# Keys in another order and V in longer runs, with one transposed tile moved from TensorE to the DMA queue in every second head

## The chip, the cores and the metric

The kernel runs on one core of a Trainium2 chip. The metric is the device time of one execution in microseconds, from the first to the last instruction of the core with what lies around them; lower is better. "TensorE", "VectorE", "ScalarE" and POOL (GpSimd) are the four engines that compute, each with a queue of its own that is worked off in order; SP (SyncE) only issues DMAs, also in order. In the profile they are PE (with PEld for the loads of weights), DVE, ACT, POOL and SP.

## What is computed

A conditioned transformer block on a sequence of 2048 rows of 640 values, bf16 in and out. Six vectors are made from a condition `c`; two of them scale and shift a layer norm ahead of each half of the block, and one gates each half's result. The first half is attention with 32 heads of 128 against a given cache of 2048 keys and values; the second mixes neighbouring rows and runs an MLP.

```python
mod = (silu(c) @ w_mod)                        # sa, ca, ga, sb, cb, gb
h = layernorm(x) * (1 + ca) + sa
q = (h @ wq)                                   # 2048 x (32 heads x 128)
p = softmax(q @ k_cache^T * 128 ** -0.5)       # per head: 2048 x 2048
x = x + ga * ((p @ v_cache) @ wo)
h = layernorm(x) * (1 + cb) + sb
x = x + gb * B(h)                              # row shifts, two matmuls, layer norms, a GELU MLP
```

The sum over keys doesn't depend on the order in which the keys are taken, so long as K, P and V agree on it. The change lies in the attention.

## The kernel before

All instructions are listed in one order by a small recorder (`Prog`); it finds, for each operation, which earlier ones it must wait for (from the keys in `r=` and `w=`) and gives each engine its part of the list, in that order. A wait therefore holds up whatever stands behind it on the same engine. DMAs named "sync" go to SP's queue, those named "gpsimd" to POOL's.

The attention is a software pipeline over 512 steps: step `s` is head `h = s // 16` and query tile `j = s % 16` (128 queries). In each step:

- TensorE multiplies the query tile with all 2048 keys, in two halves of 1024 (`qk`, L286), into the PSUM tile `Sps`. VectorE scales each half into the SBUF tile `negS` (three buffers) and takes its minimum (L559). POOL joins the two minima (L569), and ScalarE takes the exponential of 2048 scores into a P buffer, `ring<-negS` (L572). There are eight P buffers (`RPB`) and twelve for transposed P (`RPT`).
- P has to be transposed so that keys lie on partitions. For 14 of a head's 16 tiles a DMA transpose does it, issued from SP (`transpose`, L222): tiles (0,1), (4,5), (6,7), (8,9), (12,13) and (14,15) in pairs, tiles 2 and 11 alone. Tiles 3 and 10 (`PE_TILES`) are transposed by TensorE against an identity, in two halves of eight blocks, spread over the steps three and four later (`t_piece`, L253). The halves are copied out of PSUM by ScalarE (L262), except the second half of tile 3, which VectorE copies (L264, `by_dve`).
- Eleven steps behind (`PVD`; eight at the very end) TensorE multiplies transposed P with V (`pv`, L299): 16 products per tile, one per 128 keys, summed in PSUM. V is kept with a column of ones behind each 128 values, so that column 128 of the sum is the softmax's denominator. ScalarE copies two tiles' sums at once to `Of` (L550).
- Four steps further POOL takes the power -1 of four denominators (`rcp`, L440), multiplies (`norm`, L447) and sends four tiles to a scratch in DRAM with a DMA of its own (L454).
- Between these, TensorE makes the next head's queries in 20 pieces (`q_piece`, L237, copied by ScalarE at L244).

K, V and the query weights of a head are double buffered and loaded from SP's queue, between the transposes in the order of the list: K of the next head at tile 2 (a DMA transpose, L205), the weights at tile 6 (L209), V of the next head at tile 12 (L214). In V's buffer partition p holds the keys t x 128 + p, sixteen runs of 128 values at a pitch of 130.

After the attention the scratch is read back transposed (L495) and the second part of the block follows; the change doesn't touch it.

Of the kernel before, what the change touches and what calls it, by code (L numbers as in the profile page):

```python
# [115 lines left out]
def bass_adaLN_cond__mha_block_cached__mixer_s_mlp__prompt_kernel(  # L116
# [21 lines left out]
    with ExitStack() as es:  # L138
# [11 lines left out]
        if True:  # L150
            with ExitStack() as es1:
# [9 lines left out]
                kv = sb1("kv", [128, 2 * SK + 2 * NKT * 130 + 2 * KT * 128 + 2 * SQ], BF16)  # L161
                small = sb1("small", [128, 4 * NQT + 32], F32)
                hTx = sb1("hTx", [128, US], BF16)
# [4 lines left out]
                rstd = small[:, 3 * NQT:4 * NQT]  # L168
                nm0, nm1, nm, rl = [small[:, 4 * NQT + 8 * i:4 * NQT + 8 * i + 8] for i in range(4)]
                hT = hTx[:, 0:KT * SQ].rearrange("p (k q) -> p k q", k=KT)  # L170
# [3 lines left out]
                KTs = kv[:, 0:o1].rearrange("p (b s) -> p b s", b=2)  # L174
                Vaug = kv[:, o1:o2].rearrange("p (b k d) -> p b k d", b=2, k=NKT)
                wq = kv[:, o2:o3].rearrange("p (b k d) -> p b k d", b=2, k=KT)
# [26 lines left out]
                def load_k(h):  # L203
                    hb = h % 2
                    G.dma("sync", lambda e: e.dma_start_transpose(KTs[:, hb], A_k_cache[0, h]), ("k", hb), w=[("KT", hb)])  # L205

# [5 lines left out]
                def load_v(h):  # L212
                    hb = h % 2
                    G.dma("sync", lambda e: e.dma_start(Vaug[:, hb, :, 0:128], A_v_cache[0, h].rearrange("(t p) d -> p t d", p=128)),  # L214
                          ("v", hb), w=[("V", hb)])
# [49 lines left out]

                by_dve = lambda g, r: r == 1 and g % NQT == PE_TILES[0]

# [24 lines left out]
                def pv(g, half):  # L292
                    hb = (g // NQT) % 2
                    b = g % RPT
                    ob = PO[:, ((g // 2) % 2) * 512 + (g % 2) * 130:]

                    def f(t):
                        for kt in range(half * 8, half * 8 + 8):
                            ins = t.matmul(ob[:, 0:129], PTs[:, b, kt, :], Vaug[:, hb, kt, 0:129],  # L299
                                           start=(kt == 0), stop=(kt == NKT - 1))  # L300
                        return ins
                    G.op("tensor", f, r=[("PT", b, half), ("V", hb), "ones"], w=[("O", (g // 2) % 2)])

# [28 lines left out]
                if H > 1:  # L332
# [89 lines left out]
                mone = small[:, 0:4]  # L422
                G.op("gpsimd", lambda g: g.memset(mone, -1.0), w=["mone"] + [("mv", t) for t in range(NQT)])
                bank(("q", 0, NQC - 1))
# [13 lines left out]
                def rcp(gr):  # L438
                    b = gr % 2
                    G.op("gpsimd", lambda g: g.tensor_tensor(  # L440
                        out=rl[:, 4 * b:4 * b + 4], in0=Of[:].rearrange("p a z d -> p (a z) d")[:, 4 * b:4 * b + 4, 128],
                        in1=mone, op=ALU.pow),
                         r=[("Of", 2 * b), ("Of", 2 * b + 1), "mone"], w=[("rl", b)])

                def norm(gr, z):
                    b = gr % 2
                    G.op("gpsimd", lambda g: g.tensor_scalar(  # L447
                        out=On[:, b, z, :], in0=Of[:, 2 * b + z // 2, z % 2, 0:128],
                        scalar1=rl[:, 4 * b + z:4 * b + z + 1], scalar2=1.0, op0=ALU.mult, op1=ALU.mult),
                        r=[("Of", 2 * b + z // 2), ("rl", b)], w=[("On", b, z)])  # L450
# [393 lines left out]
```

## Time and profile before

| | |
|---|---|
| median of 3 runs | 1614.81 us (1610.35 to 1619.43) |
| the profiled execution | 1604.1 us, span 1602.3 us |
| mean granted TensorE clock | 0.993 |
| attention, first score reduction to last exponential | 35.5 to 1253.9 us |
| projection after it, first matmul (L631) | from 1269.6 us |
| TensorE, weight loads, VectorE, ScalarE, POOL busy | 1492.6, 963.0, 1392.5, 1288.2, 622.8 us |
| DMA queue of SP | 1,161,424 packets, 314.59 MB |

The profile is of one execution. Busy time of an engine is the union of its instructions' spans. The page cuts the span into 40 equal slices and gives a busy digit for each engine in each (9 is 90% or more); the DMA digit is the mean over 16 DMA engines, whose packets overlap, so that a share can exceed 1. A group row gives source line, engine, operation, the tiles written and read, the shape and count, then busy time and mean duration. A wait row says who waited for whom, for how long in total, how often, and the longest. A row of a stretch gives its length, then busy time and count for each engine, the granted clock, the DMA share and GB/s. A row of SP's timeline gives the start of an issue and the time for which the queue was occupied with it (merged over several: x2), not the transfer, which ends later ("to landing").

### The profile page before, as it was taken

Reading aid. Unit: us, or ns where it says so; the run is one execution under the profiler, and the core shown is the slowest. Engines: PE = TensorE matmul, PEld = TensorE weight load, DVE = VectorE, ACT = ScalarE, POOL = GpSimd, SP = SyncE. Lnnn points to the kernel's source line nnn. Section 1 sums busy time; section 2 is a strip of 40 time slices with the busy share of each in tenths; the row PEclk is TensorE's granted clock in tenths of the full one; section 3 lists DMA queues with packets and bytes.
Section 4 is the critical chain, followed back from the end, with each engine's and each line's share of the span. In section 5 each row is a group of like instructions: output and inputs, shape, how many; then the busy total and the mean of one; then the engine's idle time right before and its main releaser. Section 6 shows DMA issues by size and latency. Waiting matters only on the chain.

```text
span 1602.3 us, 34804 instructions
## 1 busy us (share of the span) xinstructions
PE 1492.6 (93%) x13978; PEld 963.0 (60%) x14231; DVE 1392.5 (87%) x2460; ACT 1288.2 (80%) x1145; POOL 622.8 (39%) x1394
## 2 busy tenths in 40 slices
PE   5799999999999999999999999999999799999998
PEld 3466666666666666666666666666666555545444
DVE  6999999999999999999999999999999266666424
ACT  4999999999999999999999999999999300055330
POOL 0144444444444444444444444444444423322000
PEclk9999999999999999999999999999999899999999
DMA  9999999999999999999999999999999994530000
GB/s 305 229 230 239 238 243 237 253 241 240 237 237 233 239 237 237 239 239 247 243 250 246 250 239 235 246 228 239 236 244 244 241 196 106 106 111 1 17 17 34
DMA packets 1167730, 333.62 MB, mean 208 GB/s; under 512 B 1148304, under 2 KB 1161552, under 8 KB 1167568
## 3 DMA queue, kind: packets, MB, share of 16 engines
q1 hardware_dynamic: 1161424, 314.59, 98.3%
q0 software_dynamic: 6144, 16.79, 3.3%
q8 instruction: 112, 1.84, 0.5%
q14 instruction: 50, 0.41, 0.1%
HBM read 43.48 MB, written 19.40 MB: 39 GB/s over the span
## 4 chain that ended last, share of the span: by engine, by line
DVE 30%; ACT 24%; PE 20%; DMA 15%; issue 10%; POOL 0%; SPq 0%; ACTq 0%; DVEq 0%
DVE negS L559 27%; ACT ring L572 19%; DMA ring<-ring 13%; PE Sps L631 8%; PE Sps L772 4%; PE Oaug L756 2%; PE QPp L756 2%; ACT ring L262 2%; ACT Of L550 2%; PE Sps L741 1%; ACT kv L244 1%; DMA ring<-in_A_x_dram 1%; DVE ring L364 1%; DMA negS<-o_scratch 1%; PE Sps L286 1%
## 5 line engine op out<-in xcount | busy, mean ns | idle before, releaser
L559 DVE TENSOR_SCALAR_CACHE_REDUCE negS<-Sps 128x1024 f32<-128x1024 f32 x1024 | 1177.2, 1220 | 22.2 <-PE Sps L286 12.5
L572 ACT ACTIVATE ring<-negS,small 128x2048 bf16<-128x2048 f32 x512 | 1011.4, 2029 | 21.9 <-DMA ring<-ring 15.7
L299 PEld LDWEIGHTS PTp<-kv,ring 128*128 128x128 bf16 x8192 | 560.0, 98 | 245.0 <-DMA ring<-ring 6.7
L286 PE MATMUL Sps<-kv 128*128 128x512 bf16 x1949 | 596.3, 383 | 62.8 <-DVE negS L559 42.9
L299 PE MATMUL PTp<-kv,ring 128*128 128x129 bf16 x8192 | 645.6, 221 | 6.5 <-DMA ring<-ring 5.6
L569 POOL TENSOR_SCALAR small<-small 128x1 f32<-128x1 f32 x512 | 145.8, 285 | 621.5 <-DVE negS L559 621.4
L286 PEld LDWEIGHTS Sps<-kv 128*128 128x128 bf16 x2048 | 124.5, 97 | 187.2 <-DVE negS L559 158.0
L447 POOL TENSOR_SCALAR On<-Of,small 128x128 bf16<-128x128 f32 x512 | 189.8, 371 | 13.0
L669 ACT COPY kv<-PTp 128x640 bf16<-128x640 bf16 x32 | 22.0, 692 | 155.0 <-PE PTp L666 154.9
L440 POOL TENSOR_TENSOR small<-Of,small 128x4 f32<-128x4 f32 x128 | 133.2, 1040 | 6.3 <-ACT Of L550 6.2
L454 POOL DMA_DIRECT2D o_scratch<-On x128 | 103.1, 806 | 40.8 <-POOL On L447 37.2
L237 PE MATMUL Oaug<-hTx,kv 128*128 128x512 bf16 x265 | 101.2, 387 | 7.9 <-ACT ring L262 4.2
L550 ACT COPY Of<-PTp 128x259 f32<-128x259 f32 x256 | 99.5, 389 | 10.5 <-PE PTp L299 10.5
L237 PE MATMUL QPp<-hTx,kv 128*128 128x512 bf16 x259 | 97.5, 381 | 2.5 <-ACT hTx L391 1.8
L559 DVE DVE_READ_ACCUMULATOR negS<-Sps 128x1 f32 x1024 | 85.4, 83 | 0.0
L612 POOL TENSOR_SCALAR On<-On 128x1 f32<-128x1 f32 x48 | 24.3, 507 | 152.9 <-DVE On L621 152.9
L639 DVE TENSOR_TENSOR ring<-Sps,mod_bc 128x640 f32<-128x640 f32 x16 | 13.2, 825 | 77.0 <-PE Sps L631 77.0
L631 PE MATMUL Sps<-wo,hTx 128*128 128x128 bf16 (+1 forms) x504 | 71.8, 304 | 5.0 <-DMA hTx<-o_scratch 4.7
L776 DVE TENSOR_TENSOR ring<-Sps,ring 128x640 f32<-128x640 f32 x16 | 13.2, 825 | 66.2 <-PE Sps L772 66.2
L631 PE MATMUL Sps<-wo,negS 128*128 128x128 bf16 (+1 forms) x504 | 69.1, 298 | 1.3 <-DMA negS<-o_scratch 0.9
L262 ACT COPY ring<-Oaug 128x1024 bf16<-128x1024 bf16 x64 | 66.2, 1034 | 0.0
L631 PEld LDWEIGHTS Sps<-wo,hTx 128*128 128x128 bf16 x512 | 40.2, 99 | 36.9 <-DMA hTx<-o_scratch 4.5
(82 smaller groups left out, 1011.2 us busy)
## 6 DMA issues: line engine op xcount, KB each, us to landing
kv<-in_A_v_cache_dram SPq DMA_DIRECT2D x32, 512.0 KB, 5.2
o_scratch<-On POOLq DMA_DIRECT2D x128, 128.0 KB, 4.5
ring<-in_A_x_dram SPq DMA_DIRECT2D x8, 640.0 KB, 4.9
kv<-in_A_wq_dram SPq DMA_DIRECT2D x32, 160.0 KB, 3.6
wo<-in_A_wo_dram SPq DMA_DIRECT2D x1, 5120.0 KB, 16.4
ring<-ring SPq DMA_TRANSPOSE x256, 7.1
ring<-in_w_mod_dram SPq DMA_DIRECT2D x1, 3200.0 KB, 13.6
out_dram<-wo SPq DMA_DIRECT2D x16, 160.0 KB, 1.8
```

The costliest lines, as they stand in the source:

```text
L237: G.op("tensor", lambda t: t.matmul(JB[jb], wq[:, hb, q, :], hT[:, q, cc * 512:(cc + 1) * 512], start=(q == 0), stop=(q == KT - 1)), r=[(" ...
L262: G.op("scalar", lambda a: a.copy(dst, src), r=[("J", jb)], w=[("PT", g % RPT, r)])
L286: ins = t.matmul(Sps[:, col:col + 512], QT[:, hb, j * 128:(j + 1) * 128], KTs[:, hb, col:col + 512], start=True, stop=True)
L299: ins = t.matmul(ob[:, 0:129], PTs[:, b, kt, :], Vaug[:, hb, kt, 0:129], start=(kt == 0), stop=(kt == NKT - 1))
L440: G.op("gpsimd", lambda g: g.tensor_tensor(out=rl[:, 4 * b:4 * b + 4], in0=Of[:].rearrange("p a z d -> p (a z) d")[:, 4 * b:4 * b + 4, 128 ...
L447: G.op("gpsimd", lambda g: g.tensor_scalar(out=On[:, b, z, :], in0=Of[:, 2 * b + z // 2, z % 2, 0:128], scalar1=rl[:, 4 * b + z:4 * b + z ...
L454: G.dma("gpsimd", lambda e: e.dma_start(o_scr[jj // 2:jj // 2 + 2, :, hh].rearrange("a p z d -> p a (z d)"), On[:, b].rearrange("p (a z) d ...
L550: G.op("scalar", lambda a, p=p: a.copy(Of[:, p % 4].rearrange("p z d -> p (z d)")[:, 0:259], PO[:, (p % 2) * 512:(p % 2) * 512 + 259]), r= ...
L559: G.op("vector", lambda v, half=half, s=s, r8=r8: v.tensor_scalar(out=negS[:, s % 3, half * 1024:(half + 1) * 1024], in0=Sps[:, half * 102 ...
L569: G.op("gpsimd", lambda g, r8=r8: g.tensor_scalar(out=nm[:, r8:r8 + 1], in0=nm0[:, r8:r8 + 1], scalar1=nm1[:, r8:r8 + 1], scalar2=None, op ...
L572: G.op("scalar", lambda a, s=s, r8=r8: a.activation(Pb[:, s % RPB, :], negS[:, s % 3, :], ACT.Exp, bias=nm[:, r8:r8 + 1], scale=-1.0), r=[ ...
L631: ins = t.matmul(YB[b][:, c0:c0 + cw], OTj[pr % 2][:, 2 * hh + z, :], wo[:, hh, c0:c0 + cw], start=(hh == 0), stop=(hh == H - 1))
```

## The change

Keys are taken in the order 16 p + c: partition p holds sixteen consecutive keys, and key tile c is the keys 16 p + c. K is transposed from a view of 128 rows of 4 KB, V is loaded in eight runs of two keys (512 bytes) per partition, at a pitch of 260 elements, with two ones ahead of each run and two behind it. Even key tiles multiply [1, V] (129 columns, starting on element 1 of the run's slot), odd ones [V, 1] with a result one column further on, so that V's sums meet in columns 1 to 128, and the sums of ones end up in two columns, 0 and 129. Because these two columns start at different products, the first key tile needs all 130 columns written: a copy of its V with a one ahead and a zero behind is kept in a small buffer `V0`, made by POOL once per head at tile 2, ahead of that step's other POOL work. POOL adds the two sums before the power.

In the odd heads tile 3 is no longer transposed by TensorE; tiles 2 and 3 go as one pair by DMA. Tile 10 stays with TensorE in all heads. VectorE copies the second half of tile 3 in every fourth head alone (0, 4, 8, ...); where TensorE transposes it in the other even heads, ScalarE copies it.

```diff
-                small = sb1("small", [128, 4 * NQT + 32], F32)
+                small = sb1("small", [128, 4 + 130 + 2 + 32], F32)
+                V0 = small[:, 4:134].bitcast(BF16).rearrange("p (b d) -> p b d", b=2)
-                Vaug = kv[:, o1:o2].rearrange("p (b k d) -> p b k d", b=2, k=NKT)
+                Vaug = kv[:, o1:o2].rearrange("p (b k d) -> p b k d", b=2, k=NKT // 2)
...
-                    G.dma("sync", lambda e: e.dma_start_transpose(KTs[:, hb], A_k_cache[0, h]), ("k", hb), w=[("KT", hb)])
+                    G.dma("sync", lambda e: e.dma_start_transpose(
+                        KTs[:, hb].rearrange("p (c q) -> p c q", c=NKT), A_k_cache[0, h].rearrange("(q c) d -> q (c d)", c=NKT)), ("k", hb), w=[("KT", hb)])
...
-                    G.dma("sync", lambda e: e.dma_start(Vaug[:, hb, :, 0:128], A_v_cache[0, h].rearrange("(t p) d -> p t d", p=128)),
+                    G.dma("sync", lambda e: e.dma_start(Vaug[:, hb, :, 2:258], A_v_cache[0, h].rearrange("(p t z) d -> p t (z d)", t=NKT // 2, z=2)),
...
-                is_pe = lambda g: g % NQT in PE_TILES
+                is_pe = lambda g: g % NQT in PE_TILES[(g // NQT) % 2:]
...
-                by_dve = lambda g, r: r == 1 and g % NQT == PE_TILES[0]
+                by_dve = lambda g, r: r == 1 and g % NQT == PE_TILES[0] and (g // NQT) % 4 == 0
...
-                            ins = t.matmul(ob[:, 0:129], PTs[:, b, kt, :], Vaug[:, hb, kt, 0:129],
+                            ins = t.matmul(ob[:, 0:130] if kt == 0 else ob[:, kt % 2:kt % 2 + 129], PTs[:, b, kt, :],
+                                           V0[:, hb] if kt == 0 else Vaug[:, hb, kt // 2, (1, 130)[kt % 2]:(130, 259)[kt % 2]],
...
-                G.op("gpsimd", lambda g: g.memset(Vaug[:, :, :, 128:130], 1.0), w=["ones"])
+                for c0 in (0, 258):
+                    G.op("gpsimd", lambda g, c0=c0: g.memset(Vaug[:, :, :, c0:c0 + 2], 1.0), w=[("ones", c0)])
...
+                G.op("gpsimd", lambda g: g.memset(V0[:, :, 0:1], 1.0), w=["v0o"] + SMK)
+                G.op("gpsimd", lambda g: g.memset(V0[:, :, 129:130], 0.0), r=["v0o"], w=["v0e"])
...
                     G.op("gpsimd", lambda g: g.tensor_tensor(
-                        out=rl[:, 4 * b:4 * b + 4], in0=Of[:].rearrange("p a z d -> p (a z) d")[:, 4 * b:4 * b + 4, 128],
-                        in1=mone, op=ALU.pow),
+                        out=rl[:, 4 * b:4 * b + 4], in0=Og[:, :, 0], in1=Og[:, :, 129], op=ALU.add),
+                         r=[("Of", 2 * b), ("Of", 2 * b + 1)], w=[("rs", b), ("rl", b)])
+                    G.op("gpsimd", lambda g: g.tensor_tensor(
+                        out=rl[:, 4 * b:4 * b + 4], in0=rl[:, 4 * b:4 * b + 4], in1=mone, op=ALU.pow),
...
+                    if s < NG and j == 2:
+                        G.op("gpsimd", lambda g, hb=h % 2: g.tensor_scalar(
+                            out=V0[:, hb, 1:129], in0=Vaug[:, hb, 0, 2:130], scalar1=1.0, scalar2=1.0, op0=ALU.mult, op1=ALU.mult),
+                            r=[("V", h % 2), "v0e"], w=[("V0", h % 2)])
...
-                            Of[:, p % 4].rearrange("p z d -> p (z d)")[:, 0:259], PO[:, (p % 2) * 512:(p % 2) * 512 + 259]),
+                            Of[:, p % 4].rearrange("p z d -> p (z d)")[:, 0:260], PO[:, (p % 2) * 512:(p % 2) * 512 + 260]),
```

More of the change, by code (lines that the diff above doesn't have):

```diff
@@ L168, in bass_adaLN_cond__mha_block_cached__mixer_s_mlp__prompt_kernel @@
                 rstd = small[:, 3 * NQT:4 * NQT]
-                nm0, nm1, nm, rl = [small[:, 4 * NQT + 8 * i:4 * NQT + 8 * i + 8] for i in range(4)]
+                nm0, nm1, nm, rl = [small[:, 136 + 8 * i:136 + 8 * i + 8] for i in range(4)]
+                V0 = small[:, 4:134].bitcast(BF16).rearrange("p (b d) -> p b d", b=2)
                 hT = hTx[:, 0:KT * SQ].rearrange("p (k q) -> p k q", k=KT)
@@ L422, in bass_adaLN_cond__mha_block_cached__mixer_s_mlp__prompt_kernel @@
                 mone = small[:, 0:4]
-                G.op("gpsimd", lambda g: g.memset(mone, -1.0), w=["mone"] + [("mv", t) for t in range(NQT)])
+                SMK = [("mv", t) for t in range(NQT)] + [("rstd", cc) for cc in range(NQC)]
+                G.op("gpsimd", lambda g: g.memset(mone, -1.0), w=["mone"] + SMK)
+                G.op("gpsimd", lambda g: g.memset(V0[:, :, 0:1], 1.0), w=["v0o"] + SMK)
+                G.op("gpsimd", lambda g: g.memset(V0[:, :, 129:130], 0.0), r=["v0o"], w=["v0e"])
                 bank(("q", 0, NQC - 1))
@@ L447, in norm @@
                     G.op("gpsimd", lambda g: g.tensor_scalar(
-                        out=On[:, b, z, :], in0=Of[:, 2 * b + z // 2, z % 2, 0:128],
+                        out=On[:, b, z, :], in0=Of[:, 2 * b + z // 2, z % 2, 1:129],
                         scalar1=rl[:, 4 * b + z:4 * b + z + 1], scalar2=1.0, op0=ALU.mult, op1=ALU.mult),
```

5 lines of the change are left out of this document (3 added, 2 removed).

## The prediction

> **What bounds the kernel now.** I read the page's head, then the same two stretches of the attention stage by engine, then the queue that issues the DMAs, then the rate of the DMA engines in short stretches, then waits and groups.
>
> The page, busy shares and DMA queues:
>
> ```profile
> PE 1492.6 (93%) x13978; PEld 963.0 (60%) x14231; DVE 1392.5 (87%) x2460; ACT 1288.2 (80%) x1145; POOL 622.8 (39%) x1394
> DMA  9999999999999999999999999999999994530000
> q1 hardware_dynamic: 1161424, 314.59, 98.3%
> q8 instruction: 112, 1.84, 0.5%
> ```
>
> Two stretches of one head each (heads 8 and 12), busy time by engine, clock, DMA share, GB/s:
>
> ```profile
> 337.70:374.90 37.20, 35.78 (x368) 24.22 (x372) 37.20 (x68) 37.20 (x32) 17.44 (x40) 1.00 1.19 245
> 488.70:527.40 38.70, 36.55 (x371) 24.89 (x376) 37.59 (x67) 36.95 (x31) 17.71 (x41) 1.00 1.26 231
> ```
>
> In head 8 VectorE and ScalarE are never idle; in head 12 both idle 1.1 to 1.8 us, and the head is longer. The first score reductions of successive heads stand 37.22 us apart in heads 1 to 9, and 37.84 on average over heads 1 to 31. So a second thing limits. SP's queue, heads 12 and 13 (start, duration):
>
> ```profile
> 525.69 6.72 SPq L222 DMA_TRANSPOSE ring<-ring  x2
> 532.46 0.59 SPq L214 DMA_DIRECT2D kv<-in_A_v_cache_dram  x1
> 533.09 18.47 SPq L222 DMA_TRANSPOSE ring<-ring  x4
> 551.61 2.01 SPq L205 DMA_TRANSPOSE kv<-in_A_k_cache_dram  x1
> 553.66 4.58 SPq L222 DMA_TRANSPOSE ring<-ring  x1
> 558.29 0.59 SPq L209 DMA_DIRECT2D kv<-in_A_wq_dram  x1
> 558.92 11.00 SPq L222 DMA_TRANSPOSE ring<-ring  x3
> ```
>
> Each row ends where the next begins (0.04 us between). The trace has this in every head from 1 on, and each transpose is issued long after the exponential that it needs: 3 to 11 us late in heads 9 to 30. From head 2's V load (issued at 112.95) to head 31's (1214.42) the queue takes 37.98 us per head and is never short of work. It sets the pace; the engines catch up and then wait:
>
> ```profile
> ACT ring L572 <- DMA ring<-ring: 15.7, 26, 1.7
> POOL small L569 <- DVE negS L559: 621.4, 508, 9.0
> DMA to landing us min/median/max: 4.5/5.2/6.3
> 535.24 0.28 POOL L569 TENSOR_SCALAR small<-small 128x1 f32<-128x1 f32 x1 [1.67 <-DVE negS L559]
> ```
>
> (The third line is the V load's, L214; the fourth is POOL's minimum for tile 2 of head 13.) What the queue's engines do in short stretches:
>
> ```profile
> 37.00:45.00 8.00, 7.17 (x34) 3.05 (x32) 3.81 (x7) 6.98 (x7) 0.59 (x2) 1.00 1.06 395
> 1288.00:1290.00 2.00, 1.96 (x33) 1.77 (x31) 0.01 (x1) 0.00 (x0) 0.00 (x0) 1.00 1.27 290
> 193.15:194.15 1.00, 1.00 (x12) 0.58 (x10) 1.00 (x3) 1.00 (x1) 0.62 (x2) 1.00 1.36 225
> 190.15:191.40 1.25, 1.25 (x13) 0.76 (x13) 1.25 (x3) 1.25 (x2) 0.65 (x3) 1.00 0.57 9
> ```
>
> These are 1280-byte packets (wo), 256-byte packets of a transpose from DRAM, 256-byte packets of a V load, and a stall of some 1.5 us just after a 16 KB instruction fetch (112 fetches in all, row q8). A tile's transpose is 524288 bytes: 1.81 us at 290 GB/s.
>
> **The change part by part.** Base: the profiled execution, 1604.1 us (span 1602.3). It is 0.7% below the median of the runs, 1614.8; I put the sum on the median. 0.5%, about what a measurement can tell, is 8 us.
>
> *Tile 3 of the 16 odd heads goes by DMA.* A single transpose (tile 2) becomes a pair (2, 3), the number of issues stays. 16 x 1.81 = +29.0 us on the queue. Upper end: the stage's own average including stalls, 38.0 us for 14 tiles, K, V and a third of a tile, 2.33 us each, +37. It can't be below 1.81, the fastest rate seen. The stalls follow instruction fetches and not bytes, so I take +29. Tile 2 now lands with tile 3, some 2 us later, while its product comes 11 tiles on and its P buffer has 2.8 us to spare in the heads that the queue limits: nothing.
>
> *V in 512-byte runs*, 1024 packets instead of 2048. Per packet and engine, 290 GB/s is 16 x 256 / 290 = 14.1 ns, 395 GB/s is 51.8 ns for 1280 bytes; the line between gives 23.5 ns at 512 and 1.51 us for a V load. Today its data move at 225 GB/s, 2.33 us, with a dip of a few tenths behind it where transposes follow a plain load, which stays. Ends: nothing saved (time goes by bytes), or 1.43 us (a 512-byte packet costs what one of 256 does, 0.90). With today's slowness kept, 1.51 x 290/225 = 1.95 us, it saves 0.38, without it 0.82; I take 0.5, as writes at a 520-byte pitch are as ragged as those at 260. 32 loads less the first, which is before the stage: -16 us (0 to -44).
> The Trainium skill, "DMA: Bandwidth & Descriptors", Specifications, asks for at least 512 B per transfer for line rate and says that below it the engine does read-modify-write. The trace shows no such step: 256-byte packets reach 290/395 = 0.73 of the rate of 1280-byte ones, which a fixed 4.7 ns per packet explains.
>
> *K.* The same 2048 packets of 256 bytes, now from rows 4 KB apart instead of 256 bytes apart. Nearest row: the transposes of the scratch (L495), rows 16 KB apart, at the full 290 GB/s; K's own are a little slower now (4.6 us to landing). -3 us (-9 to +6).
>
> *Instructions.* TensorE drops 32 per odd head (16 weight loads, 16 transposes), 512 of 28,209; at 112 fetches that is two fetches fewer, each with a stall of some 1.5 us; POOL gets 161 more. -2 us (-3 to 0).
>
> *Engine relief.* VectorE loses 24 of its 32 copies (L264, one costs 0.60 us on the chain): 14.5 us. ScalarE's 96 evacuations become 88, at 0.90 from start to start: 7 us. TensorE loses 16 x 16 transposes, some 0.9 us per tile. A head then needs 36.6 us of VectorE (64 half steps in pairs, 32 x 1.1446), and of ScalarE 36.1, 37.0 or 37.9 with two, three or four evacuations, some 36.9 on average instead of 37.2. All of it lies beside a queue that needs 38: 0. If the queue fell below 36.9 it would be worth up to 0.3 us a head, 10 us.
>
> *POOL.* 128 more additions of 128x4. The nearest rows are the 128x1 minimum (0.285 us) and the power on the same shape (1.04): I take 0.4. They hide in the 621 us in which POOL waits for VectorE; the last group stands on the end's chain: +0.4. The copies of V's first key run (32 x 0.37, as the 128x128 rows of L447) hide likewise.
>
> *The wait that is new.* The copy to V0 stands on POOL at tile 2 of each head, ahead of that tile's minimum, and reads V. Behind it wait the minimum, the exponential, then VectorE (three score buffers). V for head 13 is issued at 532.46 and lands 5.2 us later at 537.7; the minimum ran at 535.24. So POOL will stand 2 to 3 us there (1.4 us on average from head 9 by the trace, plus 0.4 for the copy). But the transposes queued on SP are 3 to 11 us behind their exponentials, so a pause of the engines drains that backlog and the queue itself never runs dry. It costs only at the end, where head 31 has no loads and the backlog runs out: +1 us (0 to +3). Without that cover it is 1.8 us in some 25 heads, +45.
>
> *Product with odd starts.* The moving V starts on odd elements, two bytes off; no row here shows that. PSUM writes move by four bytes, the first key tile has 130 columns, Of copies 260. Ends: nothing, or a quarter more on the 256 products of a head (some 60 ns each from start to start), 3.8 us, by which TensorE's 35.8 us in head 8 become 39.6. No gain is possible, since the columns stay. I take 0, as in nearly every other matmul the columns set the time.
>
> Sum: 29 - 16 - 3 - 2 + 0.4 + 1 = **+9.4 us**: 1613.5 for a profiled run like this one, **1624** on the median.
>
> **Rivals.**
> *V's small packets were the cost (faster).* If 512-byte runs end V's slowness and cost what 256-byte ones do, V saves 1.43 us: 29 - 44 - 3 - 2 + 1.4 = -19, 1596. For it: V's data are the slowest in the stage, 225 GB/s. Against: wo's packets lie on the line above. It decides once V and K together save over 0.9 us per head, half a tile. The skill's 512 B rule would put it here: at its 435 GB/s V takes 1.2 us, an estimate from that page.
> *Even.* V saves 0.82 (no slowness left) and K 0.2: 29 - 26 - 6 - 2 + 1.4 = -4, 1611.
> *POOL's wait bites.* Against it the backlog; if SP's queue shows gaps after tile 2 in each head, 1615 + 9 + 45 = 1669.
> *Odd starts cost TensorE.* TensorE then needs 39.6 us per head against 37.84 now: 31 x 1.8 = 55, 1670.
>
> **Chances and range.** The forecast's case 0.50 (its own range 1617 to 1635), V's packets 0.20, even 0.17, POOL 0.08, odd starts 0.05. The range leaves out the last two cases and reaches down to the second: 1596 to 1640; the upper end has the tiles at +37 and K at +6 with the rest as taken, 37 - 16 + 6 - 2 + 1.4 = +26. Faster than 1607: the second case and a little of the third, 0.21. Within: the rest of the third and the part of the first up to +8, 0.32. Slower: 0.47.
>
> **What would show it.** SP's rows still end to end in every head, with V-load intervals of 38.2 to 38.5 us; V's issue followed by 512-byte packets near 270 to 350 GB/s; VectorE and ScalarE less busy per head than now, with the time back as waits; POOL waiting for V at tile 2 by 1 to 3 us, with the minimum late. Wrong, if SP's queue has gaps, if heads come at 37 us or less, or if the 129-column products lengthen.

## The result, and the profile after

The changed kernel takes 1666.62 us (median of 4 runs, 1663.61 to 1669.48), the kernel before on the same chip 1612.58 (4 runs, 1610.16 to 1619.43). The ratio is 1.034 (95% interval 1.031 to 1.037): 54 us slower, where 9 were forecast, and outside the range. The direction was forecast, the size was not. The profiled execution took 1667.0 us (span 1665.2, TensorE clock 0.993 as before). One run of e10 below, 1722.78 us at a lower clock (0.968) than its other three, counts as slow and is left out; all the other runs compared here are fast ones or single runs.

The page of the changed kernel: busy shares, the DMA digits, and three DMA queues:

```profile
PE 1488.8 (89%) x13724; PEld 944.7 (57%) x13975; DVE 1386.4 (83%) x2436; ACT 1285.9 (77%) x1137; POOL 657.3 (39%) x1557
DMA  9899999999999999999999999999999996530000
q1 hardware_dynamic: 1161424, 322.97, 96.5%
q0 software_dynamic: 6144, 16.79, 3.5%
q8 instruction: 110, 1.80, 0.4%
```

TensorE, VectorE and ScalarE are busy for a smaller share than before, POOL for 34.5 us more (39% in both), and the DMA digits of the attention stay at 9 but for one 8. SP's queue moves 8.38 MB more, which is the sixteen tiles of 524288 bytes. Its number of packets is the same by coincidence: 16 tiles add 32768 packets of 256 bytes, and V's 512-byte runs take away 32 x 1024. There are two instruction fetches fewer.

SP's queue of the changed kernel in two heads, an odd one (7) and an even one (8); start of an issue and the time for which the queue was occupied with it:

```profile
312.36 0.60 SPq L216 DMA_DIRECT2D kv<-in_A_v_cache_dram  x1
313.00 16.17 SPq L224 DMA_TRANSPOSE ring<-ring  x3
329.22 3.01 SPq L206 DMA_TRANSPOSE kv<-in_A_k_cache_dram  x1
332.27 8.65 SPq L224 DMA_TRANSPOSE ring<-ring  x2
340.97 0.59 SPq L211 DMA_DIRECT2D kv<-in_A_wq_dram  x1
341.61 11.36 SPq L224 DMA_TRANSPOSE ring<-ring  x3
353.02 0.60 SPq L216 DMA_DIRECT2D kv<-in_A_v_cache_dram  x1
353.66 17.89 SPq L224 DMA_TRANSPOSE ring<-ring  x4
371.59 3.58 SPq L206 DMA_TRANSPOSE kv<-in_A_k_cache_dram  x1
375.21 4.27 SPq L224 DMA_TRANSPOSE ring<-ring  x1
379.52 0.59 SPq L211 DMA_DIRECT2D kv<-in_A_wq_dram  x1
380.17 11.10 SPq L224 DMA_TRANSPOSE ring<-ring  x3
391.31 0.60 SPq L216 DMA_DIRECT2D kv<-in_A_v_cache_dram  x1
```

The rows still stand end to end, here and in every head, and every transpose is issued after its exponential is done (by 3.7 us or more in heads 3 to 30). The queue is still never short of work, so the interval from one V load to the next is what a head costs: 40.66 us in the odd head, 38.29 in the even one. Over heads 2 to 30 the mean is 40.00 against 37.98 before, 40.82 in odd heads and 39.24 in even ones. The difference of 2.02 us in 31 heads is 62.6 us, and the span grew by 62.9, so nothing outside the queue has to be looked for. (The medians differ by less, 54, as the profiled execution before, 1604.1 us, was 8.5 us faster than the median of its kernel.)

The waits that changed (who waited for whom, us in total, times, longest), of the changed kernel:

```profile
POOL small L531 <- DMA kv<-in_A_v_cache_dram: 110.3, 30, 5.2
DVE negS L573 <- ACT ring L586: 57.6, 79, 2.3
ACT ring L586 <- DMA ring<-ring: 45.6, 54, 2.5
ACT ring L586 <- POOL small L583: 33.5, 36, 2.3
```

ScalarE waited 15.7 us for the transposes before and waits 45.6 now: the engines are relieved, and the time comes back as waiting for the queue, as the prediction has it. POOL's new wait for V is there too, 3.7 us in nearly every head.

What is not as predicted is the V load itself. A row of a stretch of 1 us: length, busy time of TensorE, its weight loads, VectorE, ScalarE and POOL, the clock, DMA share, GB/s. First the kernel before, around the V load that was issued at 762.02 and landed at 766.51 (no instruction fetch and no write to the scratch fall into it):

```profile
762.02:763.02 1.00, 1.00 (x12) 0.69 (x11) 1.00 (x3) 0.90 (x3) 0.25 (x2) 1.00 1.27 289
763.02:764.02 1.00, 1.00 (x12) 0.66 (x11) 1.00 (x3) 1.00 (x1) 0.37 (x2) 1.00 0.95 213
764.02:765.02 1.00, 1.00 (x11) 0.61 (x10) 1.00 (x3) 1.00 (x2) 0.00 (x0) 1.00 1.25 263
765.02:766.02 1.00, 1.00 (x11) 0.72 (x11) 1.00 (x1) 1.00 (x1) 0.67 (x3) 1.00 1.38 227
766.02:767.02 1.00, 0.93 (x12) 0.62 (x11) 1.00 (x3) 1.00 (x4) 0.76 (x1) 1.00 1.30 253
767.02:768.02 1.00, 1.00 (x12) 0.57 (x10) 1.00 (x3) 1.00 (x2) 0.66 (x2) 1.00 1.28 291
```

Then the changed kernel, around the load that was issued at 353.02 and landed at 358.50:

```profile
353.02:354.02 1.00, 1.00 (x11) 0.67 (x11) 1.00 (x3) 1.00 (x3) 0.00 (x0) 1.00 1.28 291
354.02:355.02 1.00, 1.00 (x12) 0.67 (x11) 1.00 (x3) 1.00 (x1) 0.62 (x2) 1.00 0.80 174
355.02:356.02 1.00, 1.00 (x12) 0.57 (x10) 1.00 (x3) 1.00 (x2) 0.00 (x0) 1.00 0.39 98
356.02:357.02 1.00, 1.00 (x12) 0.57 (x10) 1.00 (x3) 1.00 (x1) 0.00 (x0) 1.00 0.98 262
357.02:358.02 1.00, 0.93 (x11) 0.57 (x10) 1.00 (x3) 1.00 (x3) 0.00 (x0) 1.00 1.32 234
358.02:359.02 1.00, 1.00 (x12) 0.69 (x11) 1.00 (x3) 0.23 (x1) 0.44 (x2) 1.00 1.13 248
359.02:360.02 1.00, 1.00 (x12) 0.62 (x11) 1.00 (x3) 0.86 (x1) 0.70 (x3) 1.00 1.28 290
```

Against the 290 GB/s of the transposes around it, the four rows from 763 to 767 are short of 204 GB/s x us, 0.70 us of the queue; the five from 354 to 359 are short of 434, 1.50 us. The load's own 524288 bytes are 1.81 us at 290 GB/s in both. So this V load costs the queue 2.51 us before and 3.31 after. In the changed kernel the DMA engines are not even busy in the gap (share 0.39): the 512-byte packets don't take long, they come late. Once they come they are as fast as predicted: 160 to 170 of them start in the best quarters of a microsecond, some 340 GB/s, but half of a load's packets start only 3.6 us after the issue.

Two measures serve from here on. The *landing interval* of a V load goes from the landing of the DMA ahead of it on SP's queue to its own landing (mean of 30 loads). Its *queue cost* is the sum just shown, taken by packets: the time from its issue to 1.5 us after its landing, less 0.88 ns (256 bytes at 290 GB/s) for each other packet of the queue, in the loads near which no instruction fetch and no write to the scratch stands (10 to 26 of a kernel's 30 loads, in e8 only 4).

### The profile page after: what moved, and what is told of

It reads as the page before. It is cut to its first block, busy times and chain, and to the rows that moved or that the text cites. A ratio compares the mean times of both kernels' runs of the same rounds, so it can differ in the third digit from the quotient of the medians.

```text
span 1665.2 us, 34440 instructions
## 1 busy us (share of the span) xinstructions
PE 1488.8 (89%) x13724; PEld 944.7 (57%) x13975; DVE 1386.4 (83%) x2436; ACT 1285.9 (77%) x1137; POOL 657.3 (39%) x1557
## 4 chain that ended last, share of the span: by engine, by line
ACT 33%; DMA 29%; PE 19%; DVE 8%; issue 7%; POOL 2%; SPq 1%; ACTq 0%; DVEq 0%; POOLq 0%
ACT ring L586 26%; DMA ring<-ring 20%; PE Sps L645 7%; DMA kv<-in_A_v_cache_dram 7%; DVE negS L573 6%; PE Sps L786 4%; ACT ring L264 4%; ACT Of L564 2%; PE Oaug L770 2%; PE QPp L770 2%; PE Sps L755 1%; ACT kv L246 1%; SPq L224 1%; DMA ring<-in_A_x_dram 1%; DVE ring L368 1%
## 5 line engine op out<-in xcount | busy, mean ns | idle before, releaser
L586 ACT ACTIVATE ring<-negS,small 128x2048 bf16<-128x2048 f32 x512 | 1008.3, 2015 | 84.8 <-DMA ring<-ring 45.6
L301 PE MATMUL PTp<-kv,ring 128*128 128x129 bf16 x7680 | 616.4, 221 | 0.0
L301 PEld LDWEIGHTS PTp<-kv,ring 128*128 128x128 bf16 x7680 | 510.3, 98 | 176.0
L451 POOL TENSOR_TENSOR small<-small 128x4 f32<-128x4 f32 x128 | 133.2, 1040 | 10.0
L301 PE MATMUL PTp<-small,ring 128*128 128x130 bf16 x512 | 113.0, 221 | 11.8 <-DMA ring<-ring 11.6
L564 ACT COPY Of<-PTp 128x260 f32<-128x260 f32 x256 | 96.5, 377 | 12.5 <-PE PTp L301 12.4
L301 PEld LDWEIGHTS PTp<-small,ring 128*128 128x128 bf16 x512 | 50.1, 98 | 75.7 <-DMA ring<-ring 17.4
```

Source lines behind the costliest of these rows:

```text
L301: ins = t.matmul(ob[:, 0:130] if kt == 0 else ob[:, kt % 2:kt % 2 + 129], PTs[:, b, kt, :], V0[:, hb] if kt == 0 else Vaug[:, hb, kt // 2, ...
L451: G.op("gpsimd", lambda g: g.tensor_tensor(out=rl[:, 4 * b:4 * b + 4], in0=rl[:, 4 * b:4 * b + 4], in1=mone, op=ALU.pow), r=[("rs", b), "m ...
L564: G.op("scalar", lambda a, p=p: a.copy(Of[:, p % 4].rearrange("p z d -> p (z d)")[:, 0:260], PO[:, (p % 2) * 512:(p % 2) * 512 + 260]), r= ...
L586: G.op("scalar", lambda a, s=s, r8=r8: a.activation(Pb[:, s % RPB, :], negS[:, s % 3, :], ACT.Exp, bias=nm[:, r8:r8 + 1], scale=-1.0), r=[ ...
```

## The experiments

The first theory was that V's new address order or its new form makes the load dear. The rivals were the new wait on POOL, the tiles themselves at more than forecast, and the write places in SBUF. The column "before" has the kernel before, run on the same chip beside each. In the diffs, "..." stands for lines left out, and lines that are indented by two blanks show the changed argument alone.

| kernel | us | before | V-load interval | landing interval | queue cost |
|---|---|---|---|---|---|
| before | | | 37.98 | 2.64 | 2.60 |
| changed | 1666.62 | 1612.58 | 40.00 | 3.26 | 3.43 |
| e1, V0 copied later | 1660.92 | 1609.2 | 39.69 | 3.31 | 3.46 |
| e2, tile 3 alone | 1638.18 | 1609.2 | 39.05 | 2.64 | 2.71 |
| e3, key order alone | 1622.48 | 1609.2 | 38.60 | 2.94 | 2.95 |
| e4, V's runs in another order | 1642.48 | 1609.2 | 39.05 | 2.65 | 2.79 |
| e5, tiles as before | 1623.62 | 1609.98 | 38.59 | 2.82 | 3.09 |
| e6, e4 with runs of 1024 bytes | 1640.59 | 1609.98 | 38.99 | 2.67 | 2.77 |
| e7, e4 with even write places | 1645.05 | 1609.98 | 39.05 | 2.60 | 2.74 |
| e8, before with tile 2 on TensorE | 1612.32 | 1609.98 | 38.07 | 2.69 | 2.53 |
| e9, e4 with tiles as before | 1622.02 | 1610.64 | 38.51 | 2.65 | 2.81 |
| e10, changed, V on POOL's queue | 1691.73 | 1610.64 | 40.89 (K loads) | | |
| e11, before, V on POOL's queue | 1625.77 | 1610.64 | 38.48 (K loads) | | |
| e12, before, V in two loads | 1608.01 | 1610.12 | 38.17 | 2.76 (both) | |

e1 to e7 are one run each; single runs of the kernel before spread from 1605 to 1622, most of them within 5 us of the median.

**e1: is it POOL's wait?** The changed kernel with the copy to V0 at tile 8, where V has long landed.

```diff
-                    if s < NG and j == 2:
+                    if s < NG and j == 8:
```

> The changed kernel with the copy to V0 at tile 8 of each head instead of tile 2; V has long landed there and its first reader comes at tile 11. Theory (SP's DMA queue sets the pace, V's load and the extra transposes made it longer): POOL's wait for V, 110 us in the changed kernel, goes to about nothing, the exponentials wait for the transposes' buffers instead, and the time stays within 6 us of the changed kernel's 1665 (profiled). Rival (POOL's wait at tile 2 is what costs): 30 waits of 3.7 us go, and the time falls by 45 us or more, to 1620 or less.

The waits of e1 that answer to those above:

```profile
ACT ring L586 <- DMA ring<-ring: 68.3, 62, 3.2
DVE negS L573 <- ACT ring L586: 51.2, 68, 3.2
ACT ring L586 <- POOL small L583: 7.4, 13, 1.9
```

POOL's wait of 110 us for V is gone, and 1660.92 us remain: 6 us of the 54, about the size of the runs' spread. ScalarE now waits for the transposes instead (68.3). The long row "POOL waited for DMA" was covered by the queue's backlog, as predicted. In the page's chain of work V's load stands with 7% of the span, some 117 us; the chain follows what came last at each step, and taking this link away only moves the wait to the next one.

**e2: what do the tiles cost?** The kernel before with the move of tile 3 alone.

```diff
-                is_pe = lambda g: g % NQT in PE_TILES
+                is_pe = lambda g: g % NQT in PE_TILES[(g // NQT) % 2:]
...
-                by_dve = lambda g, r: r == 1 and g % NQT == PE_TILES[0]
+                by_dve = lambda g, r: r == 1 and g % NQT == PE_TILES[0] and (g // NQT) % 4 == 0
```

> The kernel before with only the move of tile 3 in the odd heads and VectorE's copy in every fourth head; K, V and POOL as before. Theory: the odd heads' queue time grows by 1.6 to 1.8 us (the changed kernel's V loads stand 1.58 us further apart over odd heads than over even ones), the even heads' stays; 16 x 1.6 to 1.8 = +25 to +29, about 1630 by a profiled run. Rival (the engines set the pace, and their relief counts): faster than before, 1590 to 1600. Rival (the tile costs all of the loss): 1660.

1638.18 against 1609.2, +29.0 us: the 16 x 1.81 of the prediction. Odd heads take 39.96 us of the queue instead of 37.74, even ones 38.20 instead of 38.21. V's load is unchanged (2.64). The term was right within what a single run can tell, and so was the step that priced the engines' relief at nothing. By the queue a tile costs rather more here than 1.81 us: 2.22 in an odd head, near the prediction's upper end of 2.33; V-load intervals are 1.07 us longer, 33 us over 31 heads. In the changed kernel odd heads take 1.58 us more than even ones.

**e3: what does the key order cost?** The kernel before with K and V read in the new order, V still in 256-byte packets (each partition's sixteen keys are neighbours in DRAM, but go to places 260 bytes apart).

```diff
-                    G.dma("sync", lambda e: e.dma_start_transpose(KTs[:, hb], A_k_cache[0, h]), ("k", hb), w=[("KT", hb)])
+                    G.dma("sync", lambda e: e.dma_start_transpose(
+                        KTs[:, hb].rearrange("p (c q) -> p c q", c=NKT), A_k_cache[0, h].rearrange("(q c) d -> q (c d)", c=NKT)), ("k", hb), w=[("KT", hb)])
...
-  A_v_cache[0, h].rearrange("(t p) d -> p t d", p=128)
+  A_v_cache[0, h].rearrange("(p t) d -> p t d", p=128)
```

> The kernel before with the key order 16 p + c alone: K from rows of 4 KB, V in the same 2048 packets of 256 bytes to the same places as before, but each partition's sixteen keys side by side in DRAM; no V0, no second column of sums. In the changed kernel a V load takes 3.3 us from the landing before it to its own, 2.6 in the kernel before. Theory A (the order of addresses in DRAM makes V slow: engines that start 32 KB apart): V takes 3.2 us or more here too, and the time grows by 31 x 0.6 to 1.3 = 20 to 40 us. Theory B (the runs of 512 bytes make it slow): V takes 2.6 us, the time stays within 6 us of before.

+13 us, between the theories' figures. With the same 2048 packets of the same size to the same places, V's landing interval goes from 2.64 to 2.94 and K's from 2.22 to 2.42. The order in which the addresses come has a price of its own, +0.30 us per V load here, half of what theory A asked for.

**e4: is it the order in the changed kernel?** The changed kernel with V's runs dealt out so that neighbouring partitions read neighbouring 512 bytes, as neighbouring partitions read neighbouring 256 bytes before.

```diff
-  A_v_cache[0, h].rearrange("(p t z) d -> p t (z d)", t=NKT // 2, z=2)
+  A_v_cache[0, h].rearrange("(t p z) d -> p t (z d)", t=NKT // 2, z=2)
```

> The changed kernel with V's runs of 512 bytes taken from DRAM so that neighbouring partitions lie side by side (run t of partition p holds the keys 256 t + 2 p and the next), everything else as changed. V's keys then don't pair with K's and P's, so the output is another sum; the work is the same. Theory A (order of addresses in DRAM): a V load takes 1.9 to 2.2 us instead of 3.3, and the time falls by 31 x 1.2 to 1.5 = 37 to 46 us, to about 1625. Theory B (the 512-byte runs, or their places in SBUF): V stays at 3.3 us and the time at 1665.

1642.48 us, 24 less than the changed kernel, and V's landing interval is back at 2.65. The number, size and places of the packets are those of the changed kernel; only the DRAM addresses' order differs. Theory A named the right cause and overrated it: it had 37 to 46 us and a load of 1.9 to 2.2. The same stretches of e4, around a load issued at 467.44 and landed at 472.27:

```profile
468.44:469.44 1.00, 0.99 (x11) 0.72 (x11) 1.00 (x1) 1.00 (x3) 0.00 (x0) 1.00 0.74 189
469.44:470.44 1.00, 1.00 (x12) 0.62 (x10) 1.00 (x3) 1.00 (x1) 0.63 (x2) 1.00 0.43 123
470.44:471.44 1.00, 1.00 (x12) 0.58 (x10) 1.00 (x3) 1.00 (x2) 0.00 (x0) 1.00 1.13 325
471.44:472.44 1.00, 1.00 (x13) 0.57 (x11) 1.00 (x3) 1.00 (x1) 0.09 (x1) 1.00 1.26 219
```

Short of 290 by 304 GB/s x us, 1.05 us, with V's own 1.81 that is 2.86. There is still a gap ahead of the packets, so even in the good order a V load of 512-byte packets costs as much of the queue as the old one of 256-byte packets, 2.79 against 2.60. The 0.5 us per load that the prediction booked as a gain is not there in either order. The first of V's packets starts 1.4 us after the issue in both, and at best as many start in a quarter of a microsecond (some 162); but half of them have started after 3.0 us in e4 and after 3.6 in the changed kernel (means of the 21 loads of each without an instruction fetch). The order slows what lies between the first packet and the full flow. e4 is 4 us above e2, which has the tiles alone.

**e5: what does all but the tiles cost?** The changed kernel with tile 3 on TensorE in every head and VectorE's copies as before (the reverse of e2's diff).

> The changed kernel with tiles 3 and 10 transposed by TensorE in all heads and VectorE's copy in every head, as before; key order, V's runs, V0 and the second column of sums as changed. Theory (the two parts add up on SP's queue): what is left is V's longer load, 0.8 us per head by the clear stretches of the two traces (2.60 and 3.43 us) up to 1.26 by the even heads, +25 to +39 against before, 1634 to 1648; heads of both parities alike. Rival (the parts hang together, since TensorE's, ScalarE's and VectorE's relief is used): slower than the changed kernel or about as slow, 1660 or more.

+13.6 us, about half of what the theory had (+25 to +39), and far from the rival's 1660. POOL waits for V in this kernel as well, and here the engines have less slack:

```profile
POOL small L531 <- DMA kv<-in_A_v_cache_dram: 98.8, 29, 4.7
...
ACT ring L586 <- POOL small L583: 23.6, 35, 1.3
```

e2 and e5 are the two halves of the change. They give 29.0 + 13.6 = 42.6 us, and the whole change 54: some 11 us appear only when both are made. By the landing intervals they are in V's load, 3.26 in the whole change against 2.82 in e5, and 0.44 x 31 is 13.6 us. Part of it may be chance of position: an instruction fetch falls between a V load's issue (or the microsecond ahead of it) and its landing in 8 of 30 loads in e5, in 5 in the changed kernel and in 16 before, and such a load's landing interval lies anywhere from 1.7 to 4.0. But the loads with no fetch and no write to the scratch differ too: their mean is 3.08 in e5 and 3.46 in the changed kernel, with 2.53 before (queue cost 3.09, 3.43 and 2.60). Why is open.

**e6 and e7: packet size and write places.** Both start from e4. e6 writes runs of four keys, 1024 bytes:

```diff
-                    G.dma("sync", lambda e: e.dma_start(Vaug[:, hb, :, 2:258], A_v_cache[0, h].rearrange("(t p z) d -> p t (z d)", t=NKT // 2, z=2)),
+                    G.dma("sync", lambda e: e.dma_start(Vaug[:, hb].rearrange("p (t k) d -> p t (k d)", k=2)[:, :, 2:514], A_v_cache[0, h].rearrange("(t p z) d -> p t (z d)", t=NKT // 4, z=4)),
...
```

e7 writes each partition's 4096 bytes without gaps, on a 64-byte boundary:

```diff
-  Vaug[:, hb, :, 2:258]
+  Vk(hb, 0, 2048).rearrange("p (t d) -> p t d", d=256)
...
```

Left out are the places of the ones in both, and in e7 the buffer, 16 elements longer, and the places from which the products and the copy to V0 read.

> As the run with V's runs side by side across partitions, with runs of four keys, 1024 bytes, 512 packets in place of 1024 of 512 bytes (sums and columns of ones are then not those of the reference). There the data came at the predicted pace of 650 packets per us once under way, but about 1.2 us passed at a quarter of that or less, so that a load cost 2.8 us of queue time. By the line through 256 and 1280 bytes the data take 1.34 us. Theory A (a run-in of fixed length ahead of V's packets): 1.2 + 1.34 = 2.5 us per load. Theory B (the run-in grows with the packet, as it did from 256 to 512 bytes): 2.8 us or more, nothing gained. Theory C (no run-in of its own): 1.5 us or less. Time 1642 less 31 x the difference.

> As the run with V's runs side by side across partitions (512 bytes), with the runs written without gaps from a 64-byte boundary on, where they lay 520 bytes apart; the columns of ones between the runs fall away, so denominators come from the first and last key tile alone, with the same instructions. If writes at ragged places slow V's load, it goes from 2.8 us to 2.2 or less and the time from 1642 to 1625 or less; if not, V stays at 2.7 to 2.9 and the time within 6 us of 1642.

Neither moves the V load: queue costs of 2.77 and 2.74, beside 2.79 in e4. That is theory B's "nothing gained" for e6, and "if not" for e7. With neighbouring partitions on neighbouring addresses the cost stays between 2.6 and 2.8 us from 256 to 512 to 1024 bytes, so it doesn't go by the number of packets; and ragged write places, which the prediction blamed for keeping half of V's slowness, cost nothing that shows. Their differences from e4, -2 and +3 us, are within the spread.

**e8: the queue relieved.** If the queue bounds the kernel before, taking bytes from it should help. Tile 2 goes to TensorE in every fourth head.

```diff
-                PE_TILES = (3, 10)
+                PE_TILES = (2, 3, 10)
...
+                is_pe = lambda g: g % NQT in PE_TILES[(g // NQT) % 4 != 3:]
...
+                by_dve = lambda g, r: r == 1 and g % NQT in PE_TILES[:2]
```

> The kernel before with the opposite of the change's move: in every fourth head tile 2 too is transposed by TensorE (four copies of P halves on ScalarE, two on VectorE there). Theory (SP's queue sets the pace at 37.98 us per head, a tile off the queue saves 1.8 to 2.2 us): the queue falls to 37.4 to 37.5, the engines need 37.9 in such a head and 37.2 in the others, 37.4 on average, so 31 x 0.45 = 10 to 17 us faster than before. Rival (the engines set the pace): 0.6 us more of VectorE and 0.9 of ScalarE in 8 heads, 5 to 7 us slower.

1612.32 us (10 runs), a ratio of 1.001 (95% interval 0.999 to 1.003): no change. Neither the theory's gain nor the rival's loss came. SP's queue now has gaps (21 us in all, 1 us before), and ScalarE's wait for transposes is down from 15.7 to 0.2 us. Stretches of e8: an ordinary head (20) and one (23) that has the third tile on TensorE:

```profile
800.70:837.90 37.20, 35.73 (x368) 24.21 (x373) 37.20 (x66) 37.20 (x33) 17.45 (x40) 1.00 1.22 230
912.40:953.40 41.00, 38.04 (x385) 26.37 (x389) 38.17 (x67) 38.62 (x33) 17.46 (x40) 0.96 1.22 240
```

In ordinary heads VectorE and ScalarE are never idle and each head takes 37.22 us; heads 3, 7, ... 27, with the extra tile, take 40.0 to 41.3. The average is back where it was. So in the kernel before the queue (37.98) and the engines (37.22) stand within 0.8 us of each other.

The dear heads aren't dear by the engines' work, though: it was to take 37.9 us, and in head 23 VectorE is busy for 38.17 and ScalarE for 38.62 of 41.00. Waits in that stretch:

```profile
ACT ring L572 <- POOL small L569: 2.3, 3, 1.4
DVE negS L559 <- PE Sps L286: 2.2, 2, 2.0
PE Oaug L253 <- ACT ring L262: 2.0, 1, 2.0
```

TensorE's next transposes wait 2.0 us for ScalarE to copy a half out of PSUM, the next scores come late, and VectorE and ScalarE idle. So e8 shows that the queue's relief was there, and that this way to get it costs as much as it brings; whether tile 2's pieces could be placed better was not tried.

**e9: both remedies.** e4's order together with the tiles as before.

> The changed kernel with the tile split (and VectorE's copies) of before, and with V's 512-byte runs read so that neighbouring partitions stand side by side in DRAM; as in e4, V's keys then don't pair with P's. It puts both remedies together. Theory (the tile step is worth 25 to 29 us, the address order of V 24, and the run length nothing): V-load intervals near 38.1 us, a V load's queue cost 2.7 to 2.8 us, time 1612 to 1618, within 0.5% of before. Rival (512-byte runs are themselves dearer than 256-byte ones, and e4 only hid it): a V load at 3.0 or more, intervals of 38.5 and 1620 or more. Third (the parts interact so that the order alone is worth the full 43 to 54 us): 1605 or less.

1622.02 us, a ratio of 1.007 (95% interval 1.004 to 1.011). V's load did what the theory said (landing interval 2.65, queue cost 2.81), the time did not: V-load intervals are 38.51 us, and 11 us remain. These two are the rival's figures, but its cause, a V load of 3.0 us or more, is not there. By landings they lie mainly in K (2.49 against 2.22 us per head, +8 us over 31 heads) and in the transposes that don't stand next to a load (14.89 against 13.86 us per head), less 0.44 us that the transposes behind V gain, and smaller gains at others. K's part is the new order of its rows, as in e3 and e5 (2.42 and 2.44). What slows the transposes is not settled; e9 has three parts of the change that e3 has not: POOL's wait for V (93.9 us), which e1 bounds at about 6 us where the queue is longer, V's 512-byte packets, and the products with V0.

**e10 and e11: another queue.** In the changed kernel and in the kernel before, V's load is issued by POOL on its own queue.

```diff
-                    G.dma("sync", lambda e: e.dma_start(Vaug
+                    G.dma("gpsimd", lambda e: e.dma_start(Vaug
```

> The changed kernel with V's load issued by POOL on its own queue instead of SP's; nothing else is changed. It asks whether the load's dear part is its place in SP's queue or its data. Theory (the 1.5 us between issue and the flow of packets is a gap in SP's queue, and the address order only lengthens it): on another queue the transposes go on meanwhile, and the load takes from the DMA engines no more than its packets need, 1.5 us at the 650 packets per us seen, instead of 3.4: V-load intervals fall from 40.0 to 38.1 us, the time by 31 x 1.9 = 59 to some 1607. Rival (the engines themselves stand still over such a load, whatever queue it is on): intervals stay at 39.5 to 40, the time at 1650 to 1667. Third (POOL's issue waits for the products that still read the buffer, and holds up the minima behind it): POOL waits for TensorE by several us per head, SP's queue shows gaps, over 1667.

> The kernel before with V's load issued by POOL on its own queue; nothing else is changed. Theory (as for e10): a load of 2.60 us leaves SP's queue and takes 1.81 us of the DMA engines (2048 packets at the 0.88 ns of a transpose's packet) or up to 2.33 (its own rate), so the queue needs 37.2 to 37.7 us per head instead of 37.98, and the engines' 37.2 to 37.8 bind: 5 to 20 us faster, 1590 to 1605. Rival (the DMA engines are lost to it on any queue): 1605 to 1615, as before. Third (POOL's issue or its wait holds up the minima; in this kernel the engines have no slack): over 1615, with ScalarE waiting for POOL.

Both are slower than their originals: e10 1691.73 us (ratio to before 1.049, 95% interval 1.043 to 1.056), e11 1625.77 (1.009, 1.006 to 1.013). The theory of a gap in SP's queue falls. Both times lie where the third theory had them, but its cause is not there: POOL doesn't wait for TensorE in the attention, SP's queue has no gaps, and in e11 ScalarE waits for POOL's minima as before (6.2 us, 5.8 before). It waits for the transposes: 31.1 us in e11, 15.7 before. In e11 the load takes 3.3 us from the transposes although it isn't in their queue: their packets start at some 263 per quarter of a microsecond until 2 us after the issue, fall to 30 between 4.5 and 4.75 us, and are back near that after 9 (mean of 29 loads; the shortfall from 2 to 9 us is 3.3 us at the rate of 263). K-load intervals go from 38.00 to 38.48. The issue also costs POOL 1.25 us, where SP had 0.58. The Trainium skill, "DMA: Bandwidth & Descriptors", Issuing engines are not separate DMA queues, says that DMAs of all issuers run on the same sixteen engines and that spreading them saves only issue time; the measurement agrees, and here it saves less than nothing. In e10 four of V's loads take 15 to 19 us to land, where the median is 7.6; during one of them, from 507 to 523 us, all DMAs together move 56 to 90 GB/s. What holds them is open.

**e12: one load or two.** The kernel before with V's load in two halves of eight key tiles, a pair of transposes between them.

```diff
-  Vaug[:, hb, :, 0:128], A_v_cache[0, h].rearrange("(t p) d -> p t d", p=128)
+  Vaug[:, hb, 8 * z:8 * z + 8, 0:128], A_v_cache[0, h, 1024 * z:1024 * z + 1024].rearrange("(t p) d -> p t d", p=128)
...
+                        if j == PVD + 3 and h + 1 < H:
+                            load_v(h + 1, 1)
```

> The kernel before with V's load of each head issued as two loads of 256 KB (the first eight key tiles, then the last eight), with one pair of transposes between them in SP's queue; same packets, same order, same total. It asks whether a plain load between transposes has a price of its own, or costs by its packets. Its 2048 packets at the 0.88 ns of a transpose's packet are 1.81 us, and its queue cost is 2.60, so the price of its own would be 0.8 us, paid twice here. Theory (a fixed price per load, the run-in between issue and flow): V-load intervals 38.7 to 38.9 us instead of 37.98, time 31 x 0.8 = 25 us longer, 1630 to 1640. Rival (the cost goes by the packets): intervals of 38.0 to 38.2, 1607 to 1617.

1608.01 us (10 runs), ratio 0.999 (95% interval 0.997 to 1.001), V-load intervals 38.17. A fixed price per load would have come twice; it didn't. The two halves have landing intervals of 1.61 and 1.15 us, 2.76 together, beside 2.64 in one. So the late start of the packets is not a toll of 0.8 us on each load. As far as this one split shows, the cost goes with the bytes that a plain load brings from DRAM between transposes; e3 and e4 show that it also goes with the order of their addresses.

No version here beats the kernel before.

## Why the prediction was wrong, step by step

- *What bounds the kernel, and the sum over the queue:* right. The queue's 2.02 us per head are the whole difference, and with the queue as the only account the experiments add up to within 11 us.
- *Tiles, +29:* right (e2, +29.0 by the time of a single run, 33 by the queue).
- *V in 512-byte runs, -16 (0 to -44):* this is the step that failed, and its sign with it. It was worked out from the price of a packet in transfers that flow steadily (23.5 ns at 512 bytes), and that price came out, 340 GB/s at the peak. But a V load's packets don't flow steadily between transposes: before they do, the queue loses 0.7 us in the old order and 1.5 in the new. The term is +0.62 us per head by the landing intervals, 19 us, and +0.83 by queue cost, 26; e4, which changes the order alone, gives 24. With +24 in place of -16 the prediction's own sum is 29 + 24 - 3 - 2 + 1.4 = +49, of 54 measured. The lower bound of the cost was set at "nothing saved", with no row behind it that excluded a loss: the step changed the order of DRAM addresses as well as the packet size, and the first was not priced at all. For K the same order was priced, by a neighbour in the trace, and for V it was overlooked.
- *The rival "V's small packets were the cost":* refuted by e4 and e6. In a good order of addresses the cost stays at 2.6 to 2.8 us from 256 to 1024 bytes. The Trainium skill, "DMA: Bandwidth & Descriptors", Specifications, asks for 512 bytes or more per transfer for line rate; for this load between transposes no run shows a gain from it.
- *K, -3 (-9 to +6):* nothing to slightly dearer. In the changed kernel K's landing interval is 1.97 to 1.99 us, but e2 has 2.01 with the old order, so the drop from 2.22 belongs to K's new neighbours in the queue. With the tiles as before the new order costs 0.2 to 0.27 us (e3, e5, e9), 6 to 8 us.
- *Instruction fetches, -2:* 112 became 110, as forecast; what that was worth was not measured.
- *Engine relief, 0:* right; VectorE and ScalarE idle more and wait for the queue. The ordinary heads of e8 show that with the engines' work of before 0.8 us per head was all that a shorter queue could win.
- *POOL's addition and V0's wait, +0.4 and +1:* the wait is longer than forecast (3.7 us in place of 1 to 3; V's median landing, 5.5 us after its issue in place of 5.2, is a small part of that), and the cover held: e1 puts it at about 6 us. The rival "POOL's wait bites" has the time of the result (1669) but not its mechanism: SP's queue shows no gaps, and without the wait 1661 us remain. A time that fits is no proof of the story that it came from.
- *Odd starts, 0:* right. The 129-column products take 221 ns after, 220 before. That rival's 1670 is as near the result as the other's 1669, and as wrong.

What stays open: why the order of addresses delays the packets (e3 and e4 show that it does, not how); why the tiles' move makes V's load another 0.44 us dearer; and what slows the transposes in e9.

## What to carry to other kernels

A DMA's price is not packets times a rate: what stands next to it on the DMA engines, and the order in which its addresses come, can matter more than the packets' size, so look at GB/s row by row around one such transfer, and price an access pattern's order as a change of its own. When a queue and the engines stand within 2% of each other, moving work between them can pay only up to the nearer of the two, and, as e8 shows, the moved work's own waits can take all of it. A long wait in the list, or a large share in the chain, is not a price; take the wait away, as e1 does, and see what takes its place.

## What had not been expected of the hardware

- The same 512 KB from DRAM, in 512-byte packets to the same places, cost SP's queue 3.4 us when each partition reads its own 4 KB and 2.8 when neighbouring partitions read neighbouring 512 bytes.
- With neighbouring partitions on neighbouring addresses, 256-, 512- and 1024-byte packets of such a load cost the queue nearly the same, 2.6 to 2.8 us, though the 512-byte ones reach 340 GB/s at their peak and the whole load's average between transposes is near 190 (524288 bytes in 2.8 us).
- A plain load on POOL's queue took no less from the transposes on SP's than one in their own queue: 3.3 us by the shortfall of their packets, beside a queue cost of 2.6.
- Moving operands that start two bytes off cost TensorE nothing that shows: 221 ns per product, 220 without.
